# Side work of a feed-forward stage ordered by keyed steps, with a second tile of 512 tokens in full products and the gated down weights kept in scratch

## The chip, the core and the metric

The kernel runs on one core of one Trainium2 chip. Its time is the device time of one launch in microseconds (us). The core's engines are named as in the profile: PE multiplies matrices (PEld is its weight load), DVE and POOL work elementwise, ACT evaluates functions and copies, SP only issues transfers. Each engine executes its own instructions in the order in which the program emitted them; engines wait for one another through semaphores.

## The reference, cut to what matters

The input is 4096 tokens of 640 features in fp32. A spectral mixing block (Fourier transform along the tokens, two small complex layers per block of features, inverse transform) is followed by a gated feed-forward block; each has a layer norm in front and is scaled and shifted by vectors made from `c`.

```python
mod = (_silu(c) @ w_mod).reshape(c.shape[0], 6, 1, -1)
sa, ca, ga, sb, cb, gb = (mod[:, i] for i in range(6))
x = x + ga * _A_ref(layernorm(x) * (1 + ca) + sa, ...)
h = layernorm(x) * (1 + cb) + sb
x = x + gb * ((silu(h @ w_gate) * (h @ w_up)) @ w_down)
```

`w_gate` and `w_up` are 640 by 1728, `w_down` is 1728 by 640. The sum is made in fp32 accuracy: every operand is split into a high part that the matrix engine holds exactly and a low rest, and a product of two operands is three matmuls (high by high, high by low, low by high).

## The kernel before

The spectral block comes first (lines 174 to 903) and leaves its result, before the last inverse transform over rows, in scratch `s2`. The feed-forward stage (lines 917 to 1737) is where the change lies.

**Tiles.** The tokens lie as 32 rows of 128. `TL` (L922) gives six tiles as (first row, half the number of rows): tiles 0 and 1 of 4 rows (512 tokens), tiles 2 to 5 of 6 rows (768 tokens). In each tile the list `STG` runs fourteen weight units and six down groups: `g p` and `u p` (gate and up, 256 columns each, p = 0 to 5), `s` and `m` for the last 192 columns, and `d p` (the down product of 256 of the 1728 rows, one unit later than its input is made; the last, `d 5`, takes the 192 left as well).

**Products.** Tile 0 is computed by `plain` (L1412): 30 matmuls of 512 columns per unit. Tiles 1 to 5 are computed by `seven` (L1464): the unit is split in two by two blocks and the two halves of the tokens, and seven block products and a remainder replace eight, in 54 matmuls of N columns, where N is half the tile's tokens: 256 in tile 1 and 384 in tiles 2 to 5. It needs sums of the activations (`h0` to `h7`, eight blocks made per pair of rows and kept in scratch `hs`) and sums of the weights (`wt`, made in tile 0 from each unit's weights by four subtractions on POOL at L1105 and two splits at L1115 and L1119, stored in scratch `td`, and loaded twice per unit by every later tile). One PSUM bank gathers three products: after each of the first three, ACT copies the bank out (`keep`, L1494: `s_x`, `s_v` for another bank, `s_y`, `s_z`), and the next product into the same bank has to wait for the copy. DVE adds a second bank to the copy (L1503); for an up unit POOL multiplies it with the gate (L1515), ACT makes the high part (`high`, L1520) and DVE the low part (`low`, L1528).

**Side work.** Beside the matmuls of tile t run: the split of the next unit's weights (`prep_w`: ACT L1079, DVE L1082); the down weights (`prep_wd`: load, two multiplications by the gate vector on POOL at L1149, ACT L1154, DVE L1158), in every tile again; and the rows of the tile after (`row_steps`, `pair_steps`): loads, POOL L1209, ACT L1213, DVE L1216, six matmuls `py` (L1224), the norm (L1243), transposes `pt` (L1265), the sums on POOL and splits into `hs`.

**Order.** All queues are written out at build time. `slot` (L1033) is called between groups of matmuls; it moves a planned clock on and runs the next steps of six chains whose engine isn't booked too far ahead. A step has an engine, a planned length and a pause; it doesn't know which buffers or results it needs. `keep`, `high`, `low` and `summed` are not in chains: `seven` emits them at fixed places, so the `high` of a unit's last block stands on ACT's queue ahead of the next unit's first `keep`. At the end of a unit what is left of the chains is flushed; loads are emitted at fixed places: `load_h` of the next tile ahead of `d 5` (L1684), `load_t` in the middle of `seven` (L1546, L1557), the down weights one group ahead (L1687 to L1690).

Of the kernel before, what the change touches and what calls it, by code (L numbers as in the profile page):

```python
# [13 lines left out]
P = 128  # L14
D = 640
# [156 lines left out]
def body(tc, x, w1, b1, w2, b2, wg, wu, wd, c, wm, k_fa, k_tb, k_tx, k_bm, k_bx, k_ga, k_ge, k_id, out, dbg=None):  # L172
# [27 lines left out]
    with ExitStack() as top:  # L200
# [716 lines left out]
        with ExitStack() as ff:  # L917
# [5 lines left out]
            NT = len(TL)  # L923
            NPR = 6
# [13 lines left out]
            hsd = [None] + [nc.dram_tensor(f"hs{t}", (P, 8, 2, 2, P * TL[t][1]), F32, kind="Internal").ap()  # L938
                            for t in range(1, NT)]
            td = nc.dram_tensor("td", (NW, 2, P, 1024), F32, kind="Internal").ap()  # L940

            early = {}

            def take(tag, shape, dt, bufs, name):
                if early.get(tag):
                    return early[tag].pop(0)
                return fp.tile(shape, dt, tag=tag, bufs=bufs, name=name)

            def place(tag, shape, dt, bufs, name):
                early.setdefault(tag, []).append(fp.tile(shape, dt, tag=tag, bufs=bufs, name=name))  # L950
# [26 lines left out]
            turn = [0]  # L977

# [5 lines left out]

            nxt = [0]

            def any_bank(name):
                nxt[0] += 1
                return bank(nxt[0] % 4, name)

            side = [0]

            def side_bank(name):
                side[0] += 1
                return bank(1 + side[0] % 3, name)

            now = [0.0]
            free = dict.fromkeys("AVPST", 0.0)  # L1000

            class Chain:
                def __init__(self):
                    self.steps, self.ready = [], 0.0

                def add(self, steps, start=0.0):
                    if not self.steps:
                        self.ready = max(self.ready, now[0] + start)
                    self.steps += steps

                def can(self):
                    return self.steps and (len(self.steps[0]) < 5 or self.steps[0][4]())

                def run(self):
                    e, n, f, pause = self.steps.pop(0)[:4]
                    f()
                    if e == "T":
                        now[0] += n
                        free[e] = now[0]
                    else:  # L1020
                        free[e] = max(free[e], now[0]) + n
                    self.ready = free[e] + pause

                def flush(self):
                    while self.steps:
                        self.run()
# [6 lines left out]
            def slot(n, hold=""):  # L1033
                now[0] += n
                for c in chains:
                    while c.can():
                        e = c.steps[0][0]
                        if e in hold or c.ready > now[0] + early[e] or free[e] > now[0] + ahead[e]:
                            break
                        c.run()  # L1040

            def core(e, n):
                free[e] = max(free[e], now[0]) + n
# [5 lines left out]
            split_done = [0]  # L1049

            def load_w(t, n):
                k, p = WG[n]
                if t == 0 and n % 3 == 1:
                    r = take("h1", [P, 5, 256], F32, 1, f"r{t}_{n}")
                else:
                    r = take("R", [P, 5, 256], F32, 2, f"r{t}_{n}")
                if k in "gu":
                    nc.sync.dma_start(r, (wgv if k == "g" else wuv)[:, :, 256 * p:256 * p + 256])
                else:
                    c, f = (P, 12 * P) if k == "m" else (64, 13 * P)  # L1060
                    nc.sync.dma_start(r[:, :, 0:c], wgv[:, :, f:f + c])
                    nc.sync.dma_start(r[:, :, c:2 * c], wuv[:, :, f:f + c])
                raw[t, n] = r

            def load_t(t, n, i):
                wt = take("wt", [P, 2, 2, 2, P], F32R, 2, f"wt{t}_{n}{i}")
                nc.sync.dma_start(f32(wt.rearrange("p a b c d -> p (a b c d)")), td[n, i])
                wts[t, n, i] = wt


            def prep_w(t, n):
                r = raw[t, n]
                wb = take("wb", [P, 2, 5, 256], F32R, 2, f"wb{t}_{n}")
                wbs[t, n] = wb
                c = P if WG[n][0] == "s" else 256
                out = []

                def high(ks, e=slice(0, c)):
                    act.activation(wb[:, 0, ks, e], r[:, ks, e], AF.Copy)  # L1079

                def low(ks, e=slice(0, c)):
                    dve.tensor_tensor(wb[:, 1, ks, e], r[:, ks, e], f32(wb[:, 0, ks, e]), op=OP.subtract)  # L1082

                for ks, x, y in ((slice(0, 2), 0.6, 0.7), (slice(2, 5), 0.85, 0.96)):
                    out += [("A", x, lambda ks=ks: high(ks), 0.1), ("V", y, lambda ks=ks: low(ks), 0.0)]
                if c == P and t:

                    e, ks = slice(P, 2 * P), slice(0, 2)
                    out.insert(0, ("P", 0.9, lambda: pool.tensor_tensor(
                        r[:, ks, e], r[:, 1:4:2, 0:P], r[:, 0:4:2, 0:P], op=OP.subtract), 0.2))  # L1090
                    out += [("A", 0.4, lambda: high(ks, e), 0.1), ("V", 0.4, lambda: low(ks, e), 0.0)]
                return out


            def sum_w(n):
                r = raw[0, n]
                ts = []
                b11, b21 = r[:, 0:4:2, 0:P], r[:, 1:4:2, 0:P]
                b12, b22 = r[:, 0:4:2, P:256], r[:, 1:4:2, P:256]

                def sub(o, a, b):
                    def f():
                        if not ts:
                            ts.append(take(f"h{6 * (n % 2)}", [P, 4, 2, P], F32, 1, f"ts{n}"))
                        pool.tensor_tensor(ts[0][:, o], a if a is not None else ts[0][:, 3],  # L1105
                                           b if not isinstance(b, int) else ts[0][:, b], op=OP.subtract)
                    return ("P", 0.9, f, 0.1) + ((lambda: split_done[0] >= n - 2,) if o == 3 else ())

                def split():
                    out = []  # L1110
                    for i in range(2):
                        def high(i=i):
                            wt = take("wt", [P, 2, 2, 2, P], F32R, 2, f"wt0_{n}{i}")
                            wts[0, n, i] = wt
                            act.activation(wt[:, :, 0], ts[0][:, 2 * i:2 * i + 2], AF.Copy)  # L1115

                        def low(i=i):
                            wt = wts[0, n, i]
                            (pool if i and n % 2 else dve).tensor_tensor(wt[:, :, 1], ts[0][:, 2 * i:2 * i + 2], f32(wt[:, :, 0]),  # L1119
                                                               op=OP.subtract)  # L1120

                        def store(i=i):
                            nc.sync.dma_start(td[n, i], f32(wts[0, n, i].rearrange("p a b c d -> p (a b c d)")))

                        out += [("A", 0.65, high, 0.1), ("P", 1.5, low, 0.3) if i and n % 2 else ("V", 0.7, low, 0.3),
                                ("S", 0.5, store, 0.0)]
                    return out + [("S", 0.0, lambda: split_done.__setitem__(0, n), 0.0)]

                return ([sub(3, b12, b11), sub(1, b22, 3), sub(0, b22, b12), sub(2, b21, 1)], split)
# [4 lines left out]
            wd_done = set()  # L1134

            def load_wd(t, p):
                w = take("wd", [P, 2, D], F32, 1, f"wdr{t}_{p}")
                if p < NPR:
                    nc.sync.dma_start(w, wd[256 * p:256 * p + 256, :].rearrange("(f p) d -> p f d", p=P))
                else:  # L1140
                    nc.sync.dma_start(w[:, 0], wd[12 * P:13 * P, :])
                    for h in range(2):
                        nc.sync.dma_start(w[64 * h:64 * h + 64, 1], wd[13 * P:F, :])
                wdraw[t, p] = w

            def prep_wd(t, p, part=(0, 1)):
# [16 lines left out]
                if 1 not in part:  # L1163
                    return
# [599 lines left out]
```

## Time and profile before

| | us |
|---|---|
| time, median of 3 runs (lowest to highest) | 1708.81 (1708.34 to 1714.34) |
| time of the profiled execution | 1705.73 |
| its span, from the first to the last instruction | 1703.7 |
| spectral block, up to the first matmul of the feed-forward stage | 334.2 |
| tile 0, 1, 2 | 185.8, 204.2, 273.8 |
| tile 3, 4, 5 | 245.2, 234.3, 226.2 |

The tiles are cut where their first unit's matmuls start. Around the cut between two tiles side work of the tile after overlaps, so a tile's own time is sharp to some us only; the sums are not touched by that. The profile gives for each stretch how long each engine was busy, the granted clock of the matrix engine (1.00 is full speed) and the share of the transfer engines in use. A row of the waits says which engine's instruction waited for which other, the total in us, how often, and the longest. PE's busy time counts a matmul up to its modelled end, about 0.17 us after the next one has started, so a busy PE may still lose time; the spacing of matmuls says more.

### The profile page before, as it was taken

Reading aid. Unit: us, or ns where it says so; the run is one execution under the profiler, and the core shown is the slowest. Engines: PE = TensorE matmul, PEld = TensorE weight load, DVE = VectorE, ACT = ScalarE, POOL = GpSimd, SP = SyncE. Lnnn points to the kernel's source line nnn. Section 1 sums busy time; section 2 is a strip of 40 time slices with the busy share of each in tenths; the row PEclk is TensorE's granted clock in tenths of the full one; section 3 lists DMA queues with packets and bytes.
Section 4 is the critical chain, followed back from the end, with each engine's and each line's share of the span. In section 5 each row is a group of like instructions: output and inputs, shape, how many; then the busy total and the mean of one; then the engine's idle time right before and its main releaser. Section 6 shows DMA issues by size and latency. Waiting matters only on the chain.

```text
span 1703.7 us, 24493 instructions
## 1 busy us (share of the span) xinstructions
PE 1494.6 (88%) x8939; PEld 1411.4 (83%) x8939; DVE 1079.1 (63%) x1944; ACT 802.3 (47%) x1606; POOL 559.0 (33%) x654
## 2 busy tenths in 40 slices
PE   7599999978896888868998979899889999998998
PEld 2499999667775887858988978899889999998998
DVE  8578887757884667645676446665367665455554
ACT  7579997543442454324454234543254443333322
POOL 5301100437472434241442243432333333213112
PEclk9799999989997998988999989999989999999999
DMA  9746456455677767685564667455766645663321
GB/s 378 271 158 194 155 183 218 127 201 186 224 233 263 272 217 228 190 297 196 183 203 154 226 242 256 146 181 177 269 223 215 190 151 176 240 221 132 137 96 71
DMA packets 206680, 344.29 MB, mean 202 GB/s; under 512 B 20640, under 2 KB 136544, under 8 KB 204512
## 3 DMA queue, kind: packets, MB, share of 16 engines
q1 hardware_dynamic: 198048, 325.19, 56.7%
q0 software_dynamic: 6928, 14.91, 2.8%
q10 hardware_dynamic: 1584, 2.62, 0.4%
q8 instruction: 70, 1.15, 0.3%
q14 instruction: 50, 0.41, 0.1%
HBM read 249.88 MB, written 83.62 MB: 196 GB/s over the span
## 4 chain that ended last, share of the span: by engine, by line
PE 38%; POOL 9%; DVE 6%; DMA 6%; ACT 5%; issue 3%; SPq 0%; POOLq 0%; ACTq 0%; DVEq 0%
PE pd L1633 17%; PE pw L1482 5%; PE pw L1484 5%; POOL sg L1515 5%; PE pw L1483 5%; DMA wdr<-in_B_w_down_dram 3%; POOL wdr L1149 3%; ACT a L1520 1%; PE pw L1488 1%; PE pw L1489 1%; PE pw L1490 1%; DVE a L1528 1%; DVE wb L1082 1%; PE py L1224 1%; ACT wb L1079 1%
## 5 line engine op out<-in xcount | busy, mean ns | idle before, releaser
L1633 PE MATMUL pd<-wdh,a 128*128 128x320 f32 x1728 | 401.1, 313 | 1.6 <-ACT wdh L1154 1.1
L1633 PEld LDWEIGHTS pd<-wdh,a 128*128 128x128 f32 x1728 | 296.4, 190 | 3.0 <-ACT wdh L1154 1.3
L1633 PE MATMUL pd<-wdl,a 128*128 128x320 f32 x896 | 278.4, 312 | 5.7 <-DVE wdl L1158 5.7
L1482 PE MATMUL pw<-h,wt 128*128 128x384 f32 (+1 forms) x520 | 186.6, 359 | 83.6 <-ACT s_x L1494 64.2
L1639 DVE TENSOR_TENSOR x<-x,pd 128x320 f32<-128x320 f32 x384 | 179.7, 484 | 121.7 <-PE pd L1633 121.2
L1528 DVE TENSOR_TENSOR a<-sg,a 128x384 fp32r<-128x384 f32 (+1 forms) x130 | 107.9, 830 | 137.1 <-ACT a L1520 137.1
L1082 DVE TENSOR_TENSOR wb<-r,wb 128x512 fp32r<-128x512 f32 (+3 forms) x173 | 152.9, 889 | 58.9 <-ACT wb L1079 57.6
L1482 PEld LDWEIGHTS pw<-h,wt 128*128 128x128 f32 x520 | 106.9, 206 | 96.4 <-ACT s_x L1494 71.2
L1149 POOL TENSOR_TENSOR wdr<-wdr,gbb 128x640 f32<-128x640 f32 x84 | 139.7, 1675 | 127.4 <-DMA wdr<-in_B_w_down_dram 117.4
L1483 PE MATMUL pw<-h,wt 128*128 128x384 f32 (+1 forms) x520 | 180.6, 347 | 0.0
L1484 PE MATMUL pw<-h,wt 128*128 128x384 f32 (+1 forms) x520 | 180.6, 347 | 0.0
L1633 PEld LDWEIGHTS pd<-wdl,a 128*128 128x128 f32 x896 | 170.5, 190 | 6.9 <-DVE wdl L1158 6.7
L1520 ACT ACTIVATE a<-sg 128x384 fp32r<-128x384 f32 (+1 forms) x130 | 65.4, 503 | 181.4 <-POOL sg L1515 181.4
L1515 POOL TENSOR_TENSOR sg<-s_x,sg 128x384 f32<-128x384 f32 (+1 forms) x30 | 39.9, 1328 | 300.6 <-DVE s_x L1503 300.6
L1482 PE MATMUL pw<-h,wb 128*128 128x384 f32 (+1 forms) x390 | 130.8, 335 | 8.2 <-ACT wb L1079 6.5
L1484 PE MATMUL pw<-h,wb 128*128 128x384 f32 (+1 forms) x390 | 129.6, 332 | 1.3 <-DVE wb L1082 1.3
L1483 PE MATMUL pw<-h,wb 128*128 128x384 f32 (+1 forms) x390 | 129.4, 332 | 0.0
L1079 ACT ACTIVATE wb<-r 128x512 fp32r<-128x512 f32 (+3 forms) x173 | 120.7, 701 | 0.2 <-DMA r<-in_B_w_gate_dram 0.2
L1484 PEld LDWEIGHTS pw<-h,wt 128*128 128x128 f32 x520 | 107.7, 207 | 0.0
L1483 PEld LDWEIGHTS pw<-h,wt 128*128 128x128 f32 x520 | 107.6, 207 | 0.0
L1494 ACT ACTIVATE s_x<-pw 128x384 f32<-128x384 f32 (+1 forms) x65 | 30.0, 461 | 163.9 <-PE pw L1484 163.9
L1488 PE MATMUL pw<-h,wb 128*128 128x384 f32 (+1 forms) x260 | 87.5, 337 | 3.1 <-ACT s_z L1494 2.3
(242 smaller groups left out, 3453.4 us busy)
## 6 DMA issues: line engine op xcount, KB each, us to landing
wt<-td SPq DMA_DIRECT2D x130, 512.0 KB, 3.3
hs<-ho SPq DMA_DIRECT2D x56, 512.0 KB, 4.2
h<-hs SPq DMA_DIRECT2D x32, 768.0 KB, 10.6
r<-in_B_w_gate_dram SPq DMA_DIRECT2D x36, 640.0 KB, 5.3
r<-in_B_w_up_dram SPq DMA_DIRECT2D x36, 640.0 KB, 5.6
wdr<-in_B_w_down_dram SPq DMA_DIRECT2D x36, 640.0 KB, 6.8
td<-wt SPq DMA_DIRECT2D x26, 512.0 KB, 3.8
g<-s SPq DMA_DIRECT2D x28, 320.0 KB, 6.8
```

Source lines behind the costliest of these rows:

```text
L1079: act.activation(wb[:, 0, ks, e], r[:, ks, e], AF.Copy)
L1082: dve.tensor_tensor(wb[:, 1, ks, e], r[:, ks, e], f32(wb[:, 0, ks, e]), op=OP.subtract)
L1149: pool.tensor_tensor(w[:, f], w[:, f], gbb, op=OP.mult)
L1482: mm(b, w(0, kp), a[:, kp, 0], start=start and kp == 0, stop=False, skip_group_check=not start)
L1483: mm(b, w(0, kp), a[:, kp, 1], start=False, stop=False, skip_group_check=not start)
L1484: mm(b, w(1, kp), a[:, kp, 0], start=False, stop=kp == 1, skip_group_check=not start)
L1488: mm(b, wb[:, 0, 4, c], AK[:, half, 0], start=False, stop=False, skip_group_check=True)
L1515: pool.tensor_tensor(sg, s, sg, op=OP.mult)
L1520: act.activation(ao[a, f][:, 0], sgs[a, 0 if k == "m" else f], AF.Copy)
L1528: dve.tensor_tensor(o[:, 1], sgs[a, 0 if k == "m" else f], f32(o[:, 0]), op=OP.subtract)
L1633: mm(pd[g, hf][:, :320], l, m, start=(i == 0), stop=(i == len(q) - 1))
L1639: dve.tensor_tensor(x2[:, e], x2[:, e], pd[g, hf][:, :320], op=OP.add)
```

## The change

`NS = 2`: tiles 0 and 1 are both computed by `plain` with 512 columns; the tile list stays. Rows of tile 1 are paired as neighbours, only the five plain blocks of activations are split and stored for it (ten splits for two pairs in place of sixteen, no sums), and it loads five blocks and no `wt`. The weight sums move: units with even n are summed in tile 0, those with odd n in tile 1, all 26 splits' low parts on DVE (seven were on POOL). Tile 2's loads of `wt` wait for the last store to `td`, and its loads of `h` for the last split of the sums, since these use the buffers of `h0`, `h1` and `h6`. The scratch `hs` is laid out so that a stored run is 512 numbers where it was 128.

The down weights are multiplied by the gate in tile 0 only, stored in scratch `wdd` (seven stores), and loaded from there, each in one piece, by tiles 1 to 5: 70 of the 84 POOL multiplications go.

Every piece of side work is a `Step` with the keys that it waits for, the key that it makes, and the buffer places that it takes and frees. The planner keeps a planned time for each key, each engine and each place; a step is emitted only when its inputs are planned to be there within a small margin. `keep` is emitted right behind its product, the chains of `high`, `low` and POOL's product are steps too (`tails`, first in the order), and an ACT step is held back if it would end over 0.45 us after the time at which the next `keep` is due (`quiet`). What PE needs is forced by `until` if it isn't there yet.

```diff
+            NS = 2
...
-            ahead = {"A": 0.6, "V": 1.2, "P": 2.0, "S": 1.5, "T": 0.1}
-            early = {"A": 0.3, "V": 0.6, "P": 0.8, "S": 0.5, "T": 0.0}
-            gate, prep, down_w, sums, parts, rows = chains = [Chain() for _ in range(6)]
...
+            EARLY = {"A": 0.1, "V": 0.3, "P": 0.3, "S": 0.3, "G": 0.3, "T": -0.25, "N": 0.0}
+            AHEAD = {"A": 0.35, "V": 0.9, "P": 1.2, "S": 0.9, "G": 1.2, "T": 0.0}
...
+            def tries(c):
+                while c.steps:
+                    st = c.steps[0]
+                    e = st.e
+                    t = c.at()
+                    if t is None or t > now[0] + EARLY[e]:
+                        return
+                    if e not in "TN":
+                        start = max(free["P" if e == "G" else e], now[0], t)
+                        if start > now[0] + AHEAD[e]:
+                            return
+                        if e == "A" and start + st.n > quiet[0] + 0.45:
+                            return
+                        if st.bulk and free["D"] > now[0] + st.bulk:
+                            return
+                    c.run()
...
+            def slot(n):
+                while n > 0:
+                    d = min(n, 0.3)
+                    now[0] += d
+                    n -= d
+                    sweep()
...
+            def until(key):
+                while key not in done:
+                    force(owner[key])
...
+            gate, prep, wld, wtl, down_w, left_l, x2_l, sums, parts, outs = [chain() for _ in range(10)]
+            rows = [chain() for _ in range(NT)]
...
+            def sum_at(n):
+                return None if WG[n][0] == "s" else n % NS
...
+                def load():
+                    w = wdraw[t, p] = take("wd", [P, 2, D], F32, 1, f"wdr{t}_{p}")
+                    if t:
+                        nc.sync.dma_start(w.rearrange("p a b -> p (a b)"), wdd[p])
...
+                for f in range(2 if t == 0 else 0):
+                    out += [Step("P", 1.65, lambda f=f: fold(f), (raw_, ("gbb", 0), ("gbb", 1)), ("wdg", p, f))]
...
+                if t == 0:
+                    out.append(Step("S", 1.7, store, (("wdf", t, p, 0), ("wdf", t, p, 1)), ("wds", p), free=("wd",)))
...
+                first_h = tuple(("tsl", n, 1) for n in range(NW) if sum_at(n) == NS - 1) + (("raw", NS - 1, NW - 1),)
...
             def summed(a, f, q, s):
...
+                    tails.append(Chain([
+                        Step("P", N / 400 + 0.15, lambda: pool.tensor_tensor(sg, s, sg, op=OP.mult),
+                             (("sum", key), ("silu", t, a, 0 if k == "m" else f)), ("mul", key), free=("s",)),
+                        Step("A", ca_ + 0.03, lambda: act.activation(o[:, 0], sg, AF.Copy), (("mul", key),), ("ah", key)),
+                        Step("V", cv_ + 0.1, lambda: dve.tensor_tensor(o[:, 1], sg, f32(o[:, 0]), op=OP.subtract),
+                             (("ah", key),), ("act", t, fc, a), free=("sg",))]))
...
+                quiet[0] = now[0] + 2 * m3
+                prod(0, 0, "B11", True)
+                s1 = keep(0, "x")
+                quiet[0] = now[0] + 2 * m3
+                need_wt(0)
+                prod(3, 6, "T3", True)
+                s7 = keep(3, "v")
...
+            LAST_T = ("td", max(n for n in range(NW) if sum_at(n) == NS - 1), 1)
...
-                    if t == 0:
-                        plain(n)
+                    if t < NS:
...
+                        plain(t, n)
```

More of the change, by code (lines that the diff above doesn't have):

```diff
@@ L983, in bank @@
                 return ps.tile([P, 512], F32, tag=f"p{q}", name=name)
+            turn = [0]
             nxt = [0]
+            side = [0]
             def any_bank(name):
                 nxt[0] += 1
-                return bank(nxt[0] % 4, name)
-            side = [0]
-            def side_bank(name):
-                side[0] += 1
[L995 to L1026, printed above, removed]
@@ L1107, in sub @@
[L1107 to L1127, printed above, removed]
@@ L1132, in body @@
+                return [sub(o) for o in (3, 1, 0, 2)], split
             wdraw = {}
             wds = {}
[L1134 to L1144, printed above, removed]
@@ L1286, in src @@
                 def src(j):
+                    if std:
+                        return [h[0][:, k] for k in range(2 * j, min(2 * j + 2, 5))]
                     return ([left_of(0, 0), left_of(1, 0)], [left_of(1, 1), h[0][:, 4]],
@@ L1326, in row_chain @@
[L1326 to L1336 removed]
+                out = row_load(r0)
@@ L1492, in keep @@
[L1492 to L1507 removed]
+                        go(3)
@@ new lines, in down @@
+                                for i, (l, m) in enumerate(s):
+                                    mm(pd[g, hf][0][:, :320], l, m, start=False, stop=i == 2)
+                                slot(0.147 * 3)
+                                put(g, hf, pd[g, hf])
+                    if last:
+                        for g in gs:
+                            out(g)
+                x = now[0] + 0.2
+                for q in [p] + ([NPR] if last else []):
+                    for tag in ("wdh", "wdl"):
+                        room[tag].append(x if t else max(x, 0.0))
```

941 lines of the change are left out of this document (593 added, 348 removed).

## The prediction

> **What bounds the kernel now.** I read the stages first: each row is a stretch, its length, then busy us (and instructions) of PE, PEld, DVE, ACT and POOL, the granted PE clock, the transfer engines' share and GB/s. Six tiles follow a block that the change doesn't touch.
>
> ```profile
> 0.00:334.20 334.20, 294.81 (x1938) 259.67 (x1938) 258.67 (x558) 253.36 (x509) 68.08 (x153) 0.96 0.62 209
> 334.20:520.00 185.80, 162.26 (x781) 136.48 (x781) 136.79 (x187) 79.90 (x142) 105.19 (x106) 0.94 0.66 218
> 520.00:724.20 204.20, 162.04 (x1127) 157.97 (x1128) 125.49 (x233) 88.48 (x202) 76.53 (x89) 0.89 0.71 232
> 724.20:998.00 273.80, 229.76 (x1298) 222.52 (x1298) 149.51 (x260) 102.07 (x203) 92.78 (x94) 0.91 0.63 210
> 998.00:1243.20 245.20, 219.90 (x1292) 216.63 (x1292) 146.61 (x257) 101.35 (x202) 84.85 (x89) 0.94 0.61 206
> 1243.20:1477.50 234.30, 216.84 (x1287) 213.74 (x1286) 144.40 (x254) 100.83 (x201) 77.35 (x83) 0.96 0.63 209
> 1477.50:1703.70 226.20, 208.98 (x1225) 204.36 (x1224) 117.64 (x196) 76.35 (x149) 54.24 (x41) 0.97 0.38 132
> ```
>
> PE leads everywhere, and no other engine is full. So I ask what PE would need without a wait, by four stretches at full clock, each cut to one kind of matmul: 384 columns (first product form), 512, 256, and down (320).
>
> ```profile
> 1477.50:1496.10 18.60, 18.60 (x108) 18.57 (x108) 3.21 (x6) 3.88 (x8) 1.00 0.60 206
> 384.80:397.60 12.80, 12.80 (x57) 10.50 (x57) 1.33 (x2) 0.58 (x1) 1.00 0.35 120
> 607.10:613.20 6.10, 6.10 (x51) 6.07 (x51) 0.42 (x1) 1.15 (x3) 1.00 0.38 141
> 1458.20:1477.50 19.30, 19.30 (x132) 19.18 (x131) 5.22 (x11) 1.00 1.02 389
> ```
>
> That is 0.172, 0.225, 0.120 and 0.146 us a matmul. A tile of 768 has 13 units of 54 and 30 more (732 x 0.172 = 126), 492 down matmuls (72), and 36 `py` and 30 `pt` (taken as down matmuls, 10): 207; the last, without row work, 198. Tile 0: 405 x 0.225 + 328 x 0.146 + 44 x 0.146 = 145. Tile 1 now: 732 x 0.120 + 48 + 10 = 145. The sum of the six is 1110 against 1369.5 spent: **259 us are lost**, 15% of the span. PE's waits in these tiles (what waited, for whom: us, times, longest) tell where:
>
> ```profile
> PE pw L1482 <- ACT s_x L1494: 64.2, 23, 4.5
> PE py L1224 <- ACT chh L1213: 25.5, 3, 11.2
> PE pt L1265 <- ACT xn L1243: 12.0, 6, 5.1
> PE pw L1482 <- ACT s_v L1494: 9.7, 5, 8.8
> PE pg L1428 <- DVE wb L1082: 8.6, 4, 3.1
> PE pw L1482 <- ACT wb L1079: 6.5, 4, 2.3
> PE pd L1633 <- DVE wdl L1158: 5.7, 4, 3.2
> PE py L1224 <- DVE chl L1216: 4.9, 3, 2.1
> PE pr L1593 <- DVE wb L1082: 4.7, 2, 3.6
> PE pw L1482 <- DMA h<-hs: 4.0, 5, 1.2
> PE pw L1482 <- ACT s_y L1494: 3.9, 3, 3.0
> ```
>
> These sum to 150. The clock loses the rest: stretch times (1 - clock) over the six rows is 11 + 22 + 25 + 15 + 9 + 7 = 89. 150 + 89 = 239 of 259; I put the other 20 down to smaller waits. Each us of waiting thus drags 89/170 = 0.52 us of half clock behind it, which I take to go with the waits. The Trainium skill, TensorE: Matmul & The Clock Gate, section What's actually happening, puts the ramp penalty under 1% of a typical kernel's span; by that at most 17 us of clock could be won in place of the 56 below, and my sum would end near 1588. This trace has 89 us, 5%, since the clock falls anew after wait upon wait.
>
> **The largest wait**, `s_x`, is an order on queues. In the last tile, with no row work:
>
> ```profile
> 1535.69 3.41 POOL L1149 TENSOR_TENSOR wdr<-wdr,gbb 128x640 f32<-128x640 f32 x2
> 1537.59 0.55 DVE L1503 TENSOR_TENSOR s_z<-pw,s_z 128x384 f32<-128x384 f32 x1
> 1539.06 1.01 POOL L1515 TENSOR_TENSOR sg<-s_z,sg 128x384 f32<-128x384 f32 x1
> 1540.03 0.99 POOL L1515 TENSOR_TENSOR sg<-s_v,sg 128x384 f32<-128x384 f32 x1
> 1541.06 0.52 ACT L1520 ACTIVATE a<-sg 128x384 fp32r<-128x384 f32 x1 [0.43 <-POOL sg L1515]
> 1541.48 0.47 ACT L1494 ACTIVATE s_x<-pw 128x384 f32<-128x384 f32 x1
> 1542.01 0.44 PE L1482 MATMUL pw<-h,wt 128*128 128x384 f32 x1 [2.04 <-ACT s_x L1494]
> ```
>
> Two gate multiplications hold POOL; the products of the finished unit come late; ACT's `high` waits for them; the next unit's copy stands behind it, and PE behind the copy. The second wait, `chh`, comes where one tile follows another:
>
> ```profile
> 969.84 16.70 DMA wdr<-in_B_w_down_dram
> 986.68 1.55 POOL wdr L1149 x2
> 989.66 1.53 POOL cr L1209
> 991.99 2.02 DVE chl L1216
> 994.05 1.70 PE py L1224 x5
> ```
>
> A down weight queued behind the next tile's `h` holds POOL's multiplication, and the row work behind it, already placed in PE's order, waits.
>
> **The change part by part.**
>
> ```profile
> L1149 POOL TENSOR_TENSOR wdr<-wdr,gbb 128x640 f32<-128x640 f32 x84 | 139.7, 1675 | 127.4 <-DMA wdr<-in_B_w_down_dram 117.4 <-ACT gbb L1187 9.9
> L1119 DVE TENSOR_TENSOR wt<-ts,wt 128x512 fp32r<-128x512 f32 x19 | 21.4, 1130 | 6.2 <-ACT wt L1115 6.2
> L1105 POOL TENSOR_TENSOR ts<-r 128x256 f32<-128x256 f32 x26 | 26.4, 1015 | 0.3 <-DMA r<-in_B_w_up_dram 0.3
> ```
>
> *Tile 1 in full products*: PE 732 x 0.120 = 88 becomes 405 x 0.225 = 91: **+3 us**, on the path (to 149). The floor is then 1114.
>
> *Gate once*: 70 x 1.675 = 117 us of POOL go in tiles 1 to 5, 23 a tile. What it is worth to PE: without it the multiplication at 1539.06 could start when `s_z` is there, 1538.14, so 0.92 of a 2.04 us wait goes, 45%; the rest is order. At tile ends the whole `chh` wait goes. Added: seven stores of 640 KB on SP in tile 0, 1.7 us each at the 389 GB/s above, beside matmuls of 145 us with the transfer engines at 0.66; without that cover 12 us. Tile 1's down loads now wait for their stores, with weight loads behind them on SP; the store lies a tile earlier, so: nothing.
>
> *Order*: `s_x` is emitted at its product, ahead of any `high`. It then waits only for an ACT step planned to end up to 0.45 us late. The nearest rows bound what is left of the three copy waits (64.2 + 9.7 + 3.9 = 78): 0, if plan and chip agree, and 43, if only POOL's share goes. I take **20**, a quarter, nearer to the first, as the cause is structural. Row work in PE's order (25.5 + 12.0 + 4.9 = 42) is now placed 0.25 us after its planned input, with no multiplication in front: between 0 and 17 (without `chh`); I take **10**. Weight splits (8.6 + 6.5 + 5.7 + 4.7 = 25) fall first in tile 0's start, which is loads and splits as before: between 11 and 25; **14**.
>
> *Sums over two tiles*: DVE in tile 0 goes from 19 splits to 12, -8 us; tile 1 gets 14 x 1.13 = 16, so at most 125 + 16 = 141 against a floor of 149. POOL in tile 1 gets 28 subtractions, 28 us, and loses 14 multiplications, 23. Both fit under PE, DVE barely. The new waits are at the step from tile 1 to 2: `h0` stands first in its chain and waits for the last split of unit `m`; all later `h` queue behind it. Eight loads of 768 KB at 389 GB/s are 16 us; tile 1's `d 5`, 88 x 0.146 = 13 us, covers them if they start with it. Between 0 and 16: I take **8**, and keep 4 of the load waits. Tile 1's own start needs five loads of 512 KB, 7 us at that rate, under tile 0's `d 5` of 13: nothing, or 7 if they start after it.
>
> *Traffic and the rest*: tile 1 loses its 26 loads of `wt`; at the lengths forecast the transfer share is 0.66 x 186/170 = 0.72 in tile 0 and 0.61 x 245/220 = 0.68 in tile 3: nothing. The longer runs in `hs`, the norm's split into two steps and the output stores are the same work off PE's path, in cover of the same matmuls: nothing.
>
> Left: 20 + 10 + 14 + 12 + 7 (of the 20 small) = 63, and 63 x 0.52 = 33 of clock, so 56 of the 89 are won. 1114 + 96 = 1210; with 334.2 the span is 1544. This execution's time was 2.0 above its span, and the median of the runs 3.1 above it: **1549 us**, 9% faster.
>
> **The rivals.** *Only POOL's share goes*: the planned lengths are off, the order is no better than before. Left: copies 43, rows 17, splits 25, loads 12, small 20 = 117, clock 61: 1114 + 178 + 334 + 5 = **1631**. For it: planned steps know no contention. 0.2.
>
> *DVE holds tiles 0 and 1*. A DVE split (min, median, max, ns) took 6.4 us beside six POOL operations, of which first and last:
>
> ```profile
> L1119 DVE TENSOR_TENSOR wt<-ts,wt x2: 679/3544/6410, 421.1 to 427.4; 128x512 fp32r<-128x512 f32 x2
> 421.24 1.58 POOL L1149 TENSOR_TENSOR wdr<-wdr,gbb 128x640 f32<-128x640 f32 x1
> 426.23 0.73 POOL L1284 TENSOR_TENSOR sa<-sa,h 128x256 f32<-128x256 f32 x1
> ```
>
> So a train of POOL work can shut DVE out until it ends; the planned lengths don't hold that, and tile 1 gets more such trains. If it decides, tiles 0 and 1 keep their 390 us in place of 294 + 48 (half of the 96): **1597**. The Trainium skill, SBUF — State Buffer, section SBUF: two separate sides, has the rule: the port pair of DVE and POOL is an exclusive lock held for an instruction. The trace agrees, and goes further: six in a row held it. Against it: POOL sheds 23 us in tile 1. 0.13.
>
> *Nearly all goes*: 20 of waits, 10 of clock: 1114 + 30 + 339 = **1483**. For it: the largest waits above are order on queues, which a plan can see. 0.12.
>
> *Slower*: the plan runs early, and ACT takes a step whose input isn't there ahead of a copy. Place: the copies of the 52 units of tiles 2 to 5. Price: 64.2/23 = 2.8 us, with clock 4.3. The forecast has about 7 such waits in it; the 160 us of gain are gone with 37 more, in 44 of 52 units (23 of 65 now); from there on it is slower. In all 52: 1549 + 45 x 4.3 = **1743**. Against it: a step is released only 0.1 us before its planned input. 0.08.
>
> **How the numbers follow.** Forecast 0.47, its own range 1515 to 1585; then 0.2, 0.13, 0.12, 0.08. Slower than 1660 are the last and the tail of the first rival; below 1475 is only a tail of the third (the floor alone is 1114 + 339 = 1453). So 1475 to 1660. About 0.5% is what a measurement of this kernel can tell from none: faster 0.90, same 0.02, slower 0.08.
>
> **What would show it.** Right: waits for `s_x` under 20 us, none of `py` for `chh` over 3 us, L1149's successor with 14 instructions, clock 0.97 or more in tiles 3 and 4 and these near 220 us; tiles 0 and 1 near 170. Wrong: waits for copies still in every second unit (first rival, or the last); DVE busy over 90% of tiles 0 and 1 at their old length; a gap over 16 us at the step to tile 2, which would say that the sums came too late; new waits for `wt` or weights behind a waiting transfer on SP.

## The result

The changed kernel takes **1489.02 us** (median; 1485.06 to 1491.52). Beside it on the same chip the kernel before took 1711.57. The ratio is 0.8694, with a 95% interval of 0.8658 to 0.8730: 13% faster. The forecast was 1549 with 1515 to 1585 for its own case; the wide range held the time, and the nearest case was the rival "nearly all goes" at 1483, which had a chance of 0.12. The profiled execution took 1486.71 us, with a span of 1484.9.

First the page of the profiled kernel after: busy time by engine, then the granted clock in 40 slices, then the chain that ended last.

```profile
PE 1421.4 (96%) x8612; PEld 1343.7 (90%) x8612; DVE 1041.5 (70%) x1890; ACT 783.4 (53%) x1519; POOL 414.7 (28%) x542
...
PEclk9799999999999999999999999999999999999999
...
PE 71%; DVE 10%; DMA 9%; ACT 5%; issue 2%; SPq 2%; POOL 1%; DVEq 0%; ACTq 0%; POOLq 0%
```

PE is busy in 96% of the span, and behind the second slice the clock is 0.9 or more in every slice. The second view holds the six tiles: stretch, its length, busy us and instructions of PE, PEld, DVE, ACT and POOL, granted clock, transfer share and GB/s.

```profile
332.90:496.20 163.30, 154.42 (x804) 133.98 (x805) 129.25 (x193) 81.67 (x140) 87.36 (x88) 0.99 0.80 267
496.20:648.00 151.80, 149.19 (x800) 132.36 (x800) 111.51 (x195) 74.99 (x135) 52.01 (x71) 1.00 0.79 273
648.00:867.80 219.80, 213.04 (x1314) 210.16 (x1313) 158.15 (x280) 110.28 (x223) 75.33 (x91) 1.00 0.74 259
867.80:1081.20 213.40, 211.31 (x1314) 210.13 (x1313) 155.16 (x276) 109.00 (x219) 70.48 (x88) 1.00 0.73 253
1081.20:1281.60 200.40, 199.49 (x1227) 199.17 (x1226) 116.63 (x197) 78.72 (x152) 31.29 (x27) 1.00 0.57 193
1281.60:1484.90 203.30, 199.59 (x1225) 198.96 (x1224) 112.12 (x194) 75.42 (x147) 29.45 (x26) 1.00 0.42 136
```

The six rows sum to 1152.0, where the kernel before spent 1369.5 and the floor is 1114. Tile 4 has 1227 PE instructions, against 1287 before, and tiles 2 and 3 have 1314: the row work of the last tiles now runs up to two tiles ahead. The third view lists PE's waits in these tiles (what waited, for whom: us, times, longest).

```profile
PE pw L1748 <- DMA wt<-td: 7.6, 9, 1.6
PE py L1401 <- DVE chl L1391: 4.8, 2, 2.6
PE pg L1673 <- DVE wb L1204: 2.3, 2, 1.4
PE pw L1748 <- ACT s_y L1767: 1.3, 1, 1.3
...
PE pw L1748 <- ACT s_x L1767: 0.4, 1, 0.4
```

The eleven rows sum to 21.5 us. They are the whole list but for one row of 0.4; of before, the eleven rows shown sum to 150 and the whole list to 166. `s_x` fell from 64.2 to 0.4, and no row-work wait for `chh` is left. The longest single wait is 2.6 us.

### The profile page after: what moved, and what is told of

It reads as the page before. It is cut to its first block, busy times and chain, and to the rows that moved or that the text cites. A ratio compares the mean times of both kernels' runs of the same rounds, so it can differ in the third digit from the quotient of the medians.

```text
span 1484.9 us, 23598 instructions
## 1 busy us (share of the span) xinstructions
PE 1421.4 (96%) x8612; PEld 1343.7 (90%) x8612; DVE 1041.5 (70%) x1890; ACT 783.4 (53%) x1519; POOL 414.7 (28%) x542
## 4 chain that ended last, share of the span: by engine, by line
PE 71%; DVE 10%; DMA 9%; ACT 5%; issue 2%; SPq 2%; POOL 1%; DVEq 0%; ACTq 0%; POOLq 0%
PE pd L1942 23%; PE pw L1748 7%; PE pw L1750 7%; PE pw L1749 7%; DMA wt<-td 4%; PE pg L1671 3%; PE pg L1672 3%; PE pg L1673 3%; PE pw L1759 2%; PE pw L1761 2%; PE pw L1760 2%; PE pc L649 2%; PE py L1401 1%; DMA hs<-ho 1%; DMA xx<-tt 1%
## 5 line engine op out<-in xcount | busy, mean ns | idle before, releaser
L1942 PE MATMUL pd<-wdh,a 128*128 128x320 f32 x1672 | 382.2, 310 | 1.4 <-DVE x L1914 0.8
L1942 PEld LDWEIGHTS pd<-wdh,a 128*128 128x128 f32 x1672 | 282.8, 188 | 2.3 <-DVE x L1914 1.0
L1748 PE MATMUL pw<-h,wt 128*128 128x384 f32 x416 | 140.8, 339 | 9.3 <-DMA wt<-td 7.6
L1295 ACT ACTIVATE wdh<-wdr 128x640 fp32r<-128x640 f32 x84 | 60.6, 734 | 153.3 <-PE pd L1942 146.1
L1750 PE MATMUL pw<-h,wt 128*128 128x384 f32 x416 | 139.2, 335 | 0.0
L1749 PE MATMUL pw<-h,wt 128*128 128x384 f32 x416 | 139.1, 334 | 0.0
L1792 POOL TENSOR_TENSOR sg<-s_x,sg 128x384 f32<-128x384 f32 x24 | 25.1, 1048 | 353.6 <-DVE s_x L1774 353.6
L1750 PE MATMUL pw<-h,wb 128*128 128x384 f32 x312 | 104.7, 336 | 0.8 <-DVE wb L1204 0.8
L1748 PE MATMUL pw<-h,wb 128*128 128x384 f32 x312 | 105.0, 336 | 0.0
L1749 PE MATMUL pw<-h,wb 128*128 128x384 f32 x312 | 104.6, 335 | 0.0
L1673 PE MATMUL pg<-ht,wb 128*128 128x512 f32 x260 | 102.2, 393 | 2.3 <-DVE wb L1204 2.3
L1671 PE MATMUL pg<-ht,wb 128*128 128x512 f32 x260 | 102.9, 396 | 1.2 <-ACT wb L1201 1.2
L1672 PE MATMUL pg<-ht,wb 128*128 128x512 f32 x260 | 102.1, 393 | 0.0
L1299 DVE TENSOR_TENSOR wdl<-wdr,wdh 128x640 fp32r<-128x640 f32 x84 | 74.7, 902 | 30.9 <-ACT wdh L1295 30.9
L1795 DVE TENSOR_TENSOR a<-sg,a 128x384 fp32r<-128x384 f32 x104 | 72.9, 709 | 31.9 <-ACT a L1794 31.2
L1748 PEld LDWEIGHTS pw<-h,wt 128*128 128x128 f32 x416 | 78.1, 188 | 12.9 <-DMA wt<-td 5.6
L1749 PEld LDWEIGHTS pw<-h,wt 128*128 128x128 f32 x416 | 78.2, 188 | 0.0
```

Of the source, the lines that this page charges most:

```text
L1299: dve.tensor_tensor(l[:, f], wdraw[t, p][:, f], f32(h[:, f]), op=OP.subtract)
L1671: mm(b, wh, hh, start=(kk == 0), stop=False)
L1672: mm(b, wh, hl, start=False, stop=False)
L1673: mm(b, wl, hh, start=False, stop=(kk == 4))
L1748: mm(b, w(0, kp), a[:, kp, 0], start=start and kp == 0, stop=False, skip_group_check=not start)
L1749: mm(b, w(0, kp), a[:, kp, 1], start=False, stop=False, skip_group_check=not start)
```

## The experiments

The first two theories were about the copies. **O**: the order on ACT's queue makes their waits, a `high` of the finished unit ahead of the next copy. **G**: POOL's gate multiplications make them, since they make that `high` late. Four runs take one part alone, twice added to the kernel before and twice taken out of the kernel after.

**Gate once, in the kernel before** (the store of the gated weights and their later loads are the only other edits):

```diff
-                if p < NPR:
+                if t:
+                    nc.sync.dma_start(w.rearrange("p a b -> p (a b)"), wdd[p])
+                elif p < NPR:
...
-                                ("P", 1.7, lambda: fold(0), 0.0), ("P", 1.7, lambda: fold(1), 0.2)])
+                    if t == 0:
+                        down_w.add([("P", 1.7, lambda: fold(0), 0.0), ("P", 1.7, lambda: fold(1), 0.2)])
```

> The kernel before with one part of the change alone: down weights gated in tile 0, stored, and loaded gated by tiles 1 to 5; the order of all else is that of before. Theory O (the order of the queues made the gain): POOL's multiplications were only 45% of a copy wait and all of the chh wait, so about (64 x 0.45 + 25) x 1.5 = 80 us go: 1630, and s_x waits stay above 30 us. Theory G (the 117 us of POOL work made the gain): 1530 or less.

Measured: 1660.35 us, ratio to before 0.9713 (0.9664 to 0.9763), 46 us of the 220. The waits of PE:

```profile
PE pw L1489 <- ACT s_x L1501: 43.1, 24, 3.1
PE py L1231 <- ACT chh L1220: 28.8, 3, 12.5
PE py L1231 <- ACT wb L1080: 13.8, 1, 13.8
```

A third of the `s_x` wait went; all four copies (`s_x`, `s_v`, `s_y`, `s_z`) together waited 80 us and wait 46 now. The `chh` wait did not go, though no multiplication stands in front of it any more after tile 0. The third row is new, and the waits for weight splits together rose from 30 to 40 us. O had forecast 1630 and G 1530 or less; both gave the multiplications too much.

**Late splits, in the kernel before**: the `high` and `low` of the last two blocks of up units 1 to 5 are emitted behind the next unit's first two copies (`later` is emptied there).

```diff
-                high(0, 1, sz)
-                low(0, 1)
-                high(1, 1, s7)
-                low(1, 1)
+                if k == "u" and p:
+                    later.extend([lambda: high(0, 1, sz), lambda: low(0, 1),
+                                  lambda: high(1, 1, s7), lambda: low(1, 1)])
...
```

> The kernel before with only the last two blocks' high and low of up units 1 to 5 emitted behind the next unit's first two copies. Theory O: s_x waits fall from 64 to 20 us or less and the time by about 45 x 1.5 = 65 us, to 1645; chh waits stay. Theory G: within 1% of before (1695 to 1725), since POOL is as full as it was.

Measured: 1659.61 us, 0.9718 (0.9666 to 0.9771), 47 us. `s_x` fell to 3.1 us, but part of the wait moved to the next copies, so that all four together still wait 51 us:

```profile
PE pw L1484 <- ACT s_y L1496: 23.9, 22, 2.7
PE pw L1490 <- ACT s_z L1496: 14.8, 7, 4.0
```

**Early splits, in the kernel after**: all open steps of a unit are written out at its end, ahead of the next unit's copies (and a unit's weights are asked for a few lines earlier, at its start).

```diff
+                for c in list(tails):
+                    while c.steps:
+                        force(c)
```

> The changed kernel, with all open tail steps (POOL's product, high, low, silu) forced out at the end of each seven-product unit, ahead of the next unit's copies, as before the change. Theory O: waits for copies return, 50 us or more in 52 units, with clock 75 or more: 1565 or slower. Theory G: below 1515, since POOL is free of multiplications and the products come early.

Measured: 1507.59 us, 0.8832 (0.8776 to 0.8887), 19 us more than the kernel after; `s_x` 2.7 us in 4 waits. Order alone does not bring the copies' waits back. Of the 12 us by which the list of waits grew, 10 are for weight splits; whether the early `high` or the earlier request for the weights makes these was not tried apart.

**Gate in every tile, in the kernel after**:

```diff
-                    if t:
-                        nc.sync.dma_start(w.rearrange("p a b -> p (a b)"), wdd[p])
-                    elif p < NPR:
+                    if p < NPR:
...
-                for f in range(2 if t == 0 else 0):
+                for f in range(2):
```

> The changed kernel, with the gate multiplied into the down weights in every tile again (70 more POOL multiplications, no stores). Theory O: the planner places them beside the matmuls: 1489 to 1510, copy waits below 10 us. Theory G: 1580 or slower, with waits for copies and for wdl.

Measured: 1502.46 us, 0.8789 (0.8743 to 0.8834), 13 us more; `s_x` 3.4 us, and here too most of what came is for weight splits (12.5 us for 4.3). Neither O nor G holds as a single cause: each part is worth 46 us where it is added alone and 13 to 19 where it is taken away alone. So the next runs combine parts and test the planner itself.

**Both parts, in the kernel before** (the two edits above together):

> The kernel before with both parts that were tried alone: the gate multiplied once, and the splits of a unit's last two blocks emitted behind the next unit's first two copies. Alone they gave 46 and 47 us. Theory I (each takes away its own waits): the gains add to 93 us less a little, 1610 to 1625 us, and the chh waits of some 28 us at the tile ends stay. Theory R (both hit the same chain, in which either late POOL work or the order makes the wait, so that only both together free it): more than the sum, 1590 us or less, with s_x, s_y and s_z together under 10 us. Theory S (both take away the same waits): less than the sum, 1635 us or more.

Measured: 1610.07 us, 0.9433 (0.9411 to 0.9455), 99 us; the parts add, 46 + 47 = 93, as theory I had it. The copies are down to 9.6 us, which R had asked for; the two largest waits left lie around the steps between tiles:

```profile
PE py L1231 <- ACT chh L1220: 29.5, 3, 12.4
PE py L1231 <- ACT wb L1080: 13.3, 1, 13.3
...
PE pw L1491 <- ACT s_x L1503: 5.2, 4, 1.8
PE pw L1491 <- ACT s_y L1503: 4.1, 6, 1.5
```

The chain that ended last, at the end of this kernel's tile 2 (start, us, what), points to a cause:

```profile
925.14 9.05 DMA h<-hs
934.20 12.89 DMA cr<-s
947.24 1.53 POOL cr L1216
948.80 0.75 ACT chh L1220
```

The row's own `cr`, of 320 KB, takes 12.9 us to come, behind eight loads of `h`.

**cr ahead of h, in the kernel before with both parts**: the first row's loads are issued ahead of the next tile's eight loads of `h`.

```diff
                             if t + 2 < NT:
                                 row_chain(t + 2)
+                                rows.run()
```

> The kernel before with gate once and late splits (1610 us), and the first row's loads of the next row work issued ahead of the eight loads of h at a tile's end, not behind them. Its chh wait stayed at 29.5 us with no multiplication left in front, and cr landed some 15 us after its issue there. Theory Q (the load of cr stands behind 6.3 MB of h in the transfer queue): the chh waits fall under 10 us, xn and chl may rise a little, and with the clock the time falls to 1575 to 1592 us. Theory B (the load waits for a buffer or its data, not for the queue): the wait stays over 20 us, 1600 to 1615 us.

Measured: 1582.92 us, 0.9275 (0.9248 to 0.9303), 27 us less than without it. `chh` is gone from the list of waits. The loads now stand the other way round, here at the end of tile 3:

```profile
1133.47 0.42 SPq L1208 DMA_DIRECT2D cr<-s  x1
1133.94 4.58 SPq L1352 DMA_DIRECT2D h<-hs  x8
1138.04 1.56 POOL L1216 TENSOR_TENSOR cr<-cr,gab 128x640 f32<-128x640 f32 x1 [1.56 <-DMA cr<-s]
```

The multiplication of `cr` starts 4.6 us after its load was issued; at the end of tile 2, the place of the chain above, it is 6.0 in place of 13.0. Theory Q holds: the queue behind `h` held the row. The change has a price: the copies' waits rise from 9.6 to 32 us and those for `h` from 3.0 to 10.5. Why the copies wait again stays open.

**One tile of full products, in the kernel after**:

```diff
-            NS = 2
+            NS = 1
```

> The kernel after with tile 1 in seven products, its weight sums and splits all made in tile 0 and loaded from scratch in tile 1. By the floors of the prediction 3 us of matmuls less; nothing else if full products change only the floor: 1483 to 1492 us. Theory T (the fifty ns matmuls of 256 columns leave the side work of a unit too little time, so that tile 1 kept part of its loss): 1500 to 1530 us, with tile 1 at 165 us or more and waits for wt or copies in it; and tile 0, with all splits, longer than its 163 us.

Measured: 1546.05 us, 0.9061 (0.9039 to 0.9083): **57 us more**, where the floors give 3 less. By tile, of this kernel (tiles 1 and 2), and its three largest PE waits (of the 24.3 us for `wt`, 18 lie in these two tiles):

```profile
497.80:676.30 178.50, 152.44 (x1127) 149.94 (x1127) 119.62 (x232) 87.94 (x201) 53.80 (x73) 0.94 0.80 266
676.30:914.00 237.70, 220.48 (x1312) 217.23 (x1313) 155.40 (x277) 109.88 (x221) 74.34 (x93) 0.95 0.74 255
```

```profile
PE pw L1748 <- DMA wt<-td: 24.3, 13, 10.6
PE pw L1748 <- issue: 8.2, 1, 8.2
PE pw L1748 <- DMA h<-hs: 6.1, 2, 4.1
```

Tile 1 is 27 us longer, tile 2 18; tiles 0, 3 and 4 are longer by 4, 8 and 6, and why stays open. The largest waits stand behind the two steps: 10.6 us for the first `wt` of tile 1, and at tile 2 the 8.2 and those for `h`. The chain at the first step has this `wt` issued at 498.93, when a load of `h` has landed, and 10.34 us on its way. Of tile 2's eight loads of `h`, seven are issued from 6 us behind the step at 676.3 on (the first fence, of this kernel); with two tiles of full products three go out 28 us ahead of the step at 648.0 and the last 11 us ahead (the second fence, of the kernel after).

```profile
667.99 1.21 SPq L1571 DMA_DIRECT2D h<-hs  x1
682.30 3.68 SPq L1571 DMA_DIRECT2D h<-hs  x7
```

```profile
620.25 1.27 SPq L1571 DMA_DIRECT2D h<-hs  x3
633.28 4.12 SPq L1571 DMA_DIRECT2D h<-hs  x5
```

Theory T's signs came (178.5 us in tile 1, waits for `wt`, a longer tile 0), its range did not; and matmuls of 256 columns stand 0.120 us apart here, not fifty ns.

**More transfers, in the kernel after**: 12 copies of 0.49 MB within HBM during tile 1, about as many bytes as a tile 1 in seven products moves more, spread over its units. The copies are extra work.

```diff
+                    if t == 1 and 0 < n < 13:
+                        nc.sync.dma_start(more[n], wd[192 * (n % 8):192 * (n % 8) + 192, :])
```

> The kernel after with 12 copies of 0.49 MB from one place of HBM to another, which nobody waits for, one in each stage of tile 1: 5.9 MB more, about what tile 1 moves more when it is made in seven products (47.5 MB against 41.4 MB in its stretch). Theory T (tile 1 is bound by transfers, so that what full products bring is the traffic that they save): tile 1 longer by 15 to 25 us, 1505 to 1515 us. Theory L (what a tile 1 in seven products loses is the late start of its first wt loads and the shorter cover of its units, not bytes): tile 1 longer by less than 5 us, 1488 to 1495 us.

Measured: 1491.26 us, 0.8731 (0.8709 to 0.8753), not to be told from the kernel after. Tile 1 took 155.2 us, 3.4 more:

```profile
500.90:656.10 155.20, 150.20 (x801) 132.37 (x801) 110.27 (x195) 74.47 (x135) 50.11 (x71) 1.00 0.86 301
```

So bytes spread over the tile are not what a tile 1 in seven products loses, and theory L is left; bytes bunched at a step were not tried. In the kernel with one tile of full products, 28 of the 45 us that PE waits in tiles 1 and 2 lie in the first 24 us behind their starts; how much of the rest is the shorter cover inside the units was not separated.

**Blind release, in the kernel after**: a step of ACT, DVE or POOL is released as soon as the steps that it needs are written out; the hold-back ahead of copies is off, and a unit's weights are asked for at its start.

```diff
-                    if t is None or t > now[0] + EARLY[e]:
+                    if t is None or e not in "AVP" and t > now[0] + EARLY[e]:
...
-                        start = max(free["P" if e == "G" else e], now[0], t)
+                        start = max(free["P" if e == "G" else e], now[0], t if e in "SG" else 0.0)
-                        if e == "A" and start + st.n > quiet[0] + 0.45:
-                            return
```

> The kernel after, in which side steps of ACT, DVE and POOL are released as soon as the steps that they need are written out, and not only when these are planned to be done; the hold-back of ACT steps ahead of a copy is off as well. Theory P (release at the planned readiness is what keeps the copies free): waits for copies come back with 40 us or more, and with their clock the time is 1550 us or more. Theory R (the steps' inputs come early enough by themselves, as copies are written out at their product and the rest only has to follow): under 1515 us, and copy waits under 15 us.

Measured: **1699.94 us**, 0.9963 (0.9939 to 0.9988): nearly the whole gain is gone, with every other part of the change in place. But not where theory P put it:

```profile
PE pw L1748 <- DMA h<-hs: 100.6, 9, 15.0
PE pw L1759 <- DMA h<-hs: 17.4, 4, 6.6
...
PE pw L1748 <- ACT s_y L1767: 8.2, 12, 2.0
...
PE pw L1748 <- ACT s_v L1767: 4.2, 3, 1.7
PE pw L1748 <- ACT s_x L1767: 3.5, 2, 2.3
```

The copies wait 19 us in all (`s_z` has 2.9 more), not 40. PE waits 118 us for `h`, at the starts of the tiles. The chain at the step to tile 3 shows why (start, us, what; the step is at 935.8):

```profile
909.36 4.58 DMA cr<-s
...
928.54 2.75 DMA hs<-ho
931.36 4.42 DMA h<-hs
935.83 0.69 PE pw L1748
...
948.83 10.03 DMA h<-hs
```

The last row of the next tile is loaded 26 us ahead of the step, so its `h` is stored and read back when PE already needs it. What holds the row work up is argued, not shown: a step that is written out early books its engine in the plan until its input is there, and rows stand last in the order. The three edits of this run were not tried apart.

**Row work as soon as written out, in the kernel after**: only PE's steps (`py`, `pt`) lose their planned start.

```diff
-                    if t is None or t > now[0] + EARLY[e]:
+                    if t is None or e != "T" and t > now[0] + EARLY[e]:
```

> The kernel after, in which the row work of PE (py and pt) is put into PE's order as soon as its inputs are written out, and not 0.25 us behind their planned end. Theory P: PE waits for chl and xn as in the kernel before, 30 to 40 us, and with clock the time is 1535 us or more. Theory R (the plan's later place hardly matters since row work is written out long before its use): under 1505 us, with waits of py and pt under 12 us.

Measured: 1494.98 us, 0.8751 (0.8729 to 0.8772), 6 us more, at the edge of what the two intervals can tell; waits for `chl` 6.9 us. The rule for PE's own steps hardly matters; what does lies among the three edits of the blind release.

**Row work one tile ahead, in the kernel after**:

```diff
-                        if held:
+                        if held or rows.index(c) > cur[0] + 1:
```

> The kernel after, in which the row work of a tile may start only in the tile ahead of it, as in the kernel before; here it runs up to two tiles ahead. All else follows the plan. Theory H (row work that is early is what takes away the waits at the tile ends: chh, xn, chl and the loads of h): 1520 us or more, with waits for h or for the row work of 15 us or more at the steps to tiles 3 to 5. Theory M (the plan places it without waits in one tile as well, and the transfers are spread more evenly, with less in tiles 1 to 3): 1475 to 1500 us.

Measured: 1488.57 us, 0.8715 (0.8692 to 0.8737): the same as the kernel after. Tile 4 gets its row work back (211.7 us for 200.4), tiles 2 and 3 are shorter by 3.8 and 1.4, and one wait of 0.8 us for `h` is left. It is not the lead of a whole tile that counts, and theory H falls.

**Both parts undone, in the kernel after** (gate in every tile, and early splits):

> The kernel after with two parts undone together that cost 13 and 18 us when undone alone: the gate is multiplied in every tile, and a unit's open splits are all written out at its end, ahead of the next unit's copies. Theory C (either part alone keeps the copies free; the 98 us that the two gave in the kernel before come back only when both are gone): 1560 us or more, with 40 us or more of waits for s_x, s_v and s_y. Theory A (the costs simply add): 1515 to 1530 us and copy waits under 12 us.

Measured: 1535.30 us, 0.8992 (0.8954 to 0.9031): 46 us more, where 13 + 19 = 32. The copies wait 20 us again, and PE waits 22 for the weight splits:

```profile
PE pw L1746 <- ACT s_x L1765: 18.8, 17, 2.8
PE pw L1746 <- ACT wb L1201: 9.9, 4, 4.5
...
PE pw L1748 <- DVE wb L1204: 6.1, 3, 3.2
```

The result lies between theories C and A. That each part covers for the other in some units would fit, but the two are worth 46 us here and 99 in the kernel before. That the plan keeps the multiplications out of the copies' way would explain the difference, and was not tried.

One path from before to after thus adds up: 1709 to 1610 with both parts, to 1583 with `cr` ahead of `h`, to 1546 with the rest of the change, to 1489 with the second tile of full products: 99 + 27 + 37 + 57 = 220. Another order of the steps would share the sum out otherwise. No run takes the new layout of `hs` alone: from the kernel at 1583 to that at 1546 the packets under 2 KB fall from 136496 to 79152 at the same 348.87 MB, and the median load of `h` lands in 8.0 us in place of 12.6. What this is worth within the 37 is open.

## Why the prediction was right, and where it was wrong

Right: that PE is the bound and its floors hold. 1152.0 is spent on a floor of 1114, and tiles 1 and 5 are within 6 us of theirs, as is tile 4 against the 198 of a tile without row work, since its own has moved ahead. Right too: that the copies' waits are late POOL work and order together, that the multiplications fall to 14, and that the transfers' share does no harm, though it rose to 0.80, not 0.72. The size was off by 60 us: 1489 lies below the forecast's own 1515 to 1585, and the range held it by way of a rival. The terms, as forecast and as the list of waits has them now:

| what is left, us | forecast | measured |
|---|---|---|
| copies | 20 | 1.7 |
| row work in PE's order | 10 | 4.8 |
| weight splits | 14 | 4.3 |
| loads | 12 | 7.6 |
| small | 7 | 3.1 |
| half clock | 33 | 2 |
| in no listed wait | 0 | 14 |
| above the floor of 1114 | 96 | 38 |

The 58 us between 96 and 38, with 1.3 of the first block, are the whole distance from 1544 to 1484.9. Point by point:

- *What is left of the waits* was mis-sized by most, 63 for 21.5. The copies have 18 of these 42 us: *20, between 0 and 43* was a choice, with no row for it, and the bound 0 was near.
- *0.52 us of clock to each us of wait*: the clock came out at 2 for 33. By the factor itself 21.5 us of waits would have cost 11, so 22 of the 31 us follow from the waits and 9 from the factor. I scaled the loss with the sum of the waits; it goes with their length (last section). The factor was also too high for before: by the records of the clock, 22 of its 89 us fall inside PE's waits, so that 150 + 89 counts them twice.
- *At tile ends the whole chh wait goes* with the multiplication: it is gone, but for another reason, so this was luck. The wait stayed at 28.8 with the gate folded once, and went when `cr` was issued ahead of `h`. The chain that I quoted showed a transfer of 16.70 us first in its row, and I took the multiplication behind it. The queue behind `h` was named there, for the down weight; the row's own `cr` stood in it too.
- *45% of the copies' wait for POOL's share*, 43 left: with the gate folded once the three copies wait 44.2 us of 78. That bound was right, though `s_x` by itself lost only 33%.
- *Tile 1 in full products: +3 us*: wrong sign. With it undone the kernel is 57 us slower. I priced the matmuls and not the starts of tiles 1 and 2 with a tile 1 in seven products. Such a tile needs eight loads of `h` and `wt` at its start, where a full one needs five loads and three of the next tile's eight went out early behind it; the waits behind the two steps bear this out for part of the 57. The 8 us that I put at the step to tile 2 were none.
- *DVE holds tiles 0 and 1*: they took 163.3 and 151.8. (The 6.4 us split of before stood beside seven POOL operations in a row, not six.) The splits that were to be shut out got shorter, 823 ns for 1130 (the row of the kernel after):

```profile
L1261 DVE TENSOR_TENSOR wt<-ts,wt 128x512 fp32r<-128x512 f32 x25 | 20.6, 823 | 2.6 <-ACT wt L1257 2.6
```

- *Only POOL's share goes* (1631): the nearest run, the kernel before with the gate once, takes 1660.
- *Slower, since the plan runs early*: the blind release shows such a price, 211 us. Its place was not the copies but the row work and `h`.
- *New waits for wt* came, 7.6 us. That they stand behind a waiting transfer on SP, as the mark said, is not shown: ahead of the longest, 1.6 us, the load was issued when PE had freed its place, and took 7.2 us.

## What to carry to other kernels

Where a schedule is written out, price a moved or reformed stage at its two steps as well as by its matmuls: count the loads that its start needs, and ask whether they can go out ahead of the step. Follow a wait past the instruction named last, to the transfer at its head and the queue that this stands in: a load may be late only because larger ones were issued ahead of it. A rule that releases side work at its planned readiness, with a hold-back ahead of what PE waits for, can be worth as much as all edits of that work together, and what it saves can lie at a tile's end and not where the waits were counted.

## What was not expected of the hardware

The loss of clock goes with the length of single waits. Over the profiles of before, after and the 12 experiments, from 334 us on, I took each PE wait with no other over 0.5 us behind it for 8 us and summed by how much the matmuls after it were spaced wider than the median of their kind. The wait itself is taken by the spacing too, which gives some 0.16 us more than the profile's idle time. After 106 waits of 1 to 2 us the median excess is 0.1 us, and 25 lost over 0.5 us. After 75 waits of 2 to 3 us it is about 1.7, and 50 lost over 0.5 us. After 59 waits of 3 us and more 57 did, mostly 1.7 to 2.8 us. The records of the clock fit: from 334 us on they stand at 0.5 for 3.41 us or a whole multiple of it at a time (but for a last one at the end of the span), and half of 3.41 is 1.7. Two stretches of 3.5 us, one of the kernel after behind a wait of 1.8 us and one of the kernel before with late splits behind a wait of 2.6:

```profile
880.80:884.30 3.50, 3.38 (x20) 3.41 (x21) 0.66 (x2) 2.00 (x5) 0.00 (x0) 1.00 0.46 180
```

```profile
1049.30:1052.80 3.50, 3.50 (x12) 3.50 (x13) 3.46 (x7) 1.99 (x4) 0.46 (x1) 0.54 0.14 26
```

The first has 20 matmuls at a clock of 1.00, the second 12 at 0.54. The Trainium skill, TensorE: Matmul & The Clock Gate, section What's actually happening, puts the ramp penalty under 1% of a typical kernel's span; it says so where it treats the warm-up of a run of matmuls, not of many waits. The loss in the kernel after stays within that, about 2 us of 1484.9 in the tiles; in the kernel before, with 89 of 1703.7, it does not. From 334 us on PE waited for over 2 us 41 times before and twice after.
